# Six heads of V instead of four kept on chip, and FFN weights read in three column blocks, in a one-core decode layer with its gradients

## The chip, the cores and the metric

The kernel runs on one core of one Trainium2 chip. The core has five engines that run side by side, each with its own queue of instructions in a fixed order: TensorE (PE), VectorE (DVE), ScalarE (ACT), GpSimd (POOL) and SyncE (SP). DMA transfers are issued from the queues of SP, POOL or ACT and are carried by 16 DMA engines that all queues share. The metric is the device time of one execution in microseconds; the time before is the median of ten runs.

## What is computed

One token (x, 448 wide) passes through an attention block over a KV cache and then a gated feed-forward block (FFN). The outputs are the layer's result and the gradients of all its inputs.

```python
W = min(4096, max(256, Sk // 4))               # the last 4096 of 32768 cache rows
q = layernorm(x) @ wq                           # 16 heads of 256, 8 KV heads
k, v = k_cache[:, :, Sk-W:, :], v_cache[:, :, Sk-W:, :]
o = softmax(q @ k.T / 16) @ v
h = x + o @ wo
g, u = layernorm(h) @ w_gate, layernorm(h) @ w_up
h2 = h + (g * u) @ w_down
# outputs: h2, and d/d(x, k_cache, v_cache, wq, wo, w_gate, w_up, w_down)
```

The gradients of k_cache and v_cache have the full shape (8, 32768, 256). Rows outside the window are zero and have to be written as zeros: 112 pieces of 2 MiB in all. That is most of what the kernel writes.

## The kernel before

All working memory is one tile, `arena`, cut by hand into overlapping views (L47-85). Views with the same bytes are used at different times, and the framework turns each overlap into a wait. The framework also decides the order of instructions in each engine's queue: it may move an instruction ahead of others in the program where its inputs allow it, but on the engine the order is then fixed, so an instruction that waits holds everything behind it.

**Zero fills.** 103 transfers of 2 MiB are issued by POOL from the very start (L113-119), all from one 16 KB-per-partition buffer of zeros (`zeros`, two halves that are cleared at L87 and L88). Each fill sends 128 rows of 16,384 bytes. Eight fills are in flight at a time: the next is issued when the oldest has landed. Another 18.9 MB of zeros (`late_jobs`, L112) go out on SP's queue at the end, from a buffer that first held V (L589, L610-613).

**First loop** (L256-324), over the 8 KV heads: K and V of a head (2 MiB each, 128 rows of 16 KB) are loaded on SP's queue. `scores` transposes K and forms the softmax; `moments` scales K by the probabilities on DVE (L298), multiplies it with V (L302, into `M_sb`), and sums the attention output (L306). There are three K slots and four V slots (`HELD = 4`); after the loop, V of heads 4 to 7 is still in the slots.

**Middle.** `wo` is loaded whole once K's slots are free (L323), the FFN weights behind it (L326-328, in one piece each, rows of 10,752 and 1,792 bytes); `w_down` was loaded near the start (L194) and its products with the incoming gradient were formed in the first loop (L218). Then attention output (L347), second layernorm (L350), gate and up (L354-357), the spread of the FFN gradient over all partitions (L372-377, into `dg_bc`), products of the weights with it on DVE (L387, L390), the backward layernorm, 32 products with `wo` (L412), and the gradient of the queries, spread into `dq_bc` (L453-458).

**Second loop** (L528-608), over heads in the order 4 5 6 7 0 1 2 3: transposes of V (L243, copies L534 and L536), then the gradients of V and K, which PE forms in pieces (L574), and ACT and DVE copy into staging slots (L578-582); two stores of 2 MiB on SP's queue follow (L584). There are three staging slots, and each round takes two. V of heads 0 to 3 is loaded again in this loop (L539, L541). The weight gradients are put into `wst` buffers on DVE (`outer`, L467, and `outer_B`, L496-497) and stored on SP's queue, spread over the rounds by `plan` (L523). `wq` is loaded a second time (L543-544) and multiplied with `dq_bc` in round 5 (L593, L596), which gives the gradient of x.

A width of 448 is no multiple of 128. The kernel lays 384 rows over 128 partitions and the other 64 rows over 128 half rows (`wqA`/`wqB`, `wg_sb`/`wgB_sb`, `par_f`, `pair_f`, `half_f`).

Of the kernel before, what the change touches and what calls it, by code (L numbers as in the profile page):

```python
# [7 lines left out]
bf16 = mybir.dt.bfloat16  # L8
f32 = mybir.dt.float32
# [4 lines left out]
D = 448  # L14
H = 16
# [5 lines left out]
FH = F // 2  # L21
NB = 7
# [3 lines left out]
ZW = 8192  # L26
NZ = (Sk - W) * Dh // (128 * ZW)
HELD = 4
# [4 lines left out]
def kernel(  # L33
# [12 lines left out]

    VB = 16 * KB  # L47
    MB = VB + HELD * 16 * KB
    RB = MB + 32 * KB
    TOTAL = RB + 81 * KB + 128  # L50
# [4 lines left out]

    zeros = ar(0, ZW)
    V_slot = [ar(VB + 16 * KB * i, T * Dh).rearrange("p (t d) -> p t d", d=Dh) for i in range(HELD)]
    M_sb = [ar(MB + 4 * KB * g, 4 * KB).bitcast(f32).rearrange("p (v h d) -> p v h d", v=2, h=2) for g in range(G)]
    wqA = ar(MB, 24 * KB).rearrange("p (c j) -> p c j", c=3)
    wqB = ar(MB + 24 * KB, 4 * KB)  # L60
    K_slot = [ar(RB + o * KB, T * Dh).rearrange("p (t d) -> p t d", d=Dh) for o in (16, 32, 0)]
    KT_slot = [ar(RB + (48 + 2 * i) * KB, 2 * KB).rearrange("p (e t k) -> p e t k", t=4, e=2) for i in range(3)]
    pK_slot = [ar(RB + (54 + 4 * i) * KB, 4 * KB).rearrange("p (t h d) -> p t h d", t=4, h=2) for i in range(2)]
    wo_sb = ar(RB, 28 * KB).rearrange("p (j n) -> p j n", n=D)
    wg_sb = [ar(RB + 28 * KB + 6272 * i, 3 * F).rearrange("p (c f) -> p c f", c=3) for i in range(2)]
    wgB_sb = [ar(RB + 28 * KB + 6272 * i + 3 * F, FH) for i in range(2)]
    junk = ar(RB + 105 * KB // 2, F)
    o_rows = junk[0:H, 0:2 * Dh].bitcast(f32)
    om = junk[:, 2 * Dh:4 * Dh].bitcast(f32).rearrange("p (a j) -> p a j", a=8)
    h_row = ar(RB + 119 * KB // 2, 2 * D)[0:1].bitcast(f32)  # L70
    diag = ar(RB + 56 * KB, F)
    wd_sb = ar(RB + 62 * KB, 2 * NB * D).rearrange("p (h b n) -> p h b n", h=2, b=NB)
    dg_bc = ar(RB + 62 * KB + 6272, 2 * F).rearrange("p (i f) -> p i f", i=2)
    junk0 = ar(RB + 62 * KB + 6272, D)
    ppad = [ar(RB + 62 * KB + 6272 + 512 * (i + 1), T * H).rearrange("p (t h) -> p t h", h=H) for i in range(2)]
    rows1, rows2 = [ar(o, 2 * KB)[0:16].bitcast(f32) for o in (RB + 62 * KB + 6272 + 1536, RB + 70 * KB)]
    ok_rows = ar(RB + 62 * KB + 6272 + 2560, 2 * KB)[0:H].bitcast(f32).rearrange("p (k d) -> p k d", k=2)
    stage = [ar(RB + 16 * KB * i, T * Dh).rearrange("p (t d) -> p t d", d=Dh) for i in range(3)]
    Rbig = [ar(o, 8 * KB).rearrange("p (l n) -> p l n", l=8) for o in (RB + 48 * KB, MB + 24 * KB)]
    VT_slot = [ar(RB + (56 + 2 * i) * KB, 2 * KB).rearrange("p (e t k) -> p e t k", t=4, e=2) for i in range(3)]  # L80
    dq_bc = ar(RB + 62 * KB, H * Dh)
    Zr = ar(RB + 72 * KB, KB).rearrange("p (w k i) -> p w k i", w=4, k=32)
    wst = [ar(MB + 12 * KB * i, 12 * KB) for i in range(2)]
    wq2A = ar(VB + 2 * 16 * KB, 24 * KB).rearrange("p (c j) -> p c j", c=3)
    wq2B = ar(VB + 2 * 16 * KB + 24 * KB, 4 * KB)
# [5 lines left out]
    wq_A = A_wq[0:384, :].rearrange("(p c) j -> p c j", c=3)  # L91
    wq_B = A_wq[384:D, :].rearrange("r (h j) -> (r h) j", h=2)
    LD.dma_start(out=wqA, in_=wq_A)
    LD.dma_start(out=wqB, in_=wq_B)
# [16 lines left out]

    late_jobs = [(out_2, G - 1, 5, 7, 2 * ZW), (out_3, G - 1, 0, 6, 2 * ZW), (out_3, G - 1, 6, 7, ZW)]  # L112
    for g in range(G):  # L113
        for o in (out_2, out_3):
            if g == G - 1 and o is out_3:
                continue
            reg = zero_rows(o, g, 0, 5 if g == G - 1 else NZ, ZW)
            for i in range(reg.shape[0]):
                ZQ.dma_start(out=reg[i], in_=zeros)  # L119


    pair_f = const.tile([128, 64], f32)
    nc.vector.reduce_sum(out=pair_f[:], in_=ident_f[:].rearrange("p (m w) -> p m w", w=2), axis=AX)
    par_f = const.tile([128, 2], f32)
    nc.vector.reduce_sum(out=par_f[:], in_=ident_f[:].rearrange("p (m w) -> p w m", w=2), axis=AX)
# [8 lines left out]
    half_f = const.tile([128, 4], f32)  # L134
    nc.vector.memset(half_f[:, 0:3], 1.0)
    nc.vector.memset(half_f[:, 3:4], 0.5)
# [5 lines left out]

    def to_columns(row, dt, out_ps, name):
        dup = small.tile([1, 128], dt, tag="dup" + name, bufs=1)
        nc.vector.tensor_copy(out=dup[:].rearrange("o (m w) -> o m w", w=2), in_=row[:, 384:D].unsqueeze(2).to_broadcast([1, 64, 2]))
        one = ones_bf if dt == bf16 else ones_f
        for c in range(3):
            nc.tensor.matmul(out_ps[:, c:c + 1], lhsT=row[:, c:384:3], rhs=one[0:1, 0:1], start=True, stop=True)
        nc.tensor.matmul(out_ps[:, 3:4], lhsT=dup[:], rhs=one[0:1, 0:1], start=True, stop=True)

    def layernorm(row, dt, name):
# [6 lines left out]
        ps = ps_t.tile([128, 6], f32, tag="tmp")  # L158
        to_columns(row, dt, ps, name)
        nc.tensor.matmul(ps[:, 4:6], lhsT=ones_f[0:1, 0:128], rhs=mv[:, 0:2], start=True, stop=True)  # L160
        xc = const.tile([128, 6], f32, tag=name + "xc")
        nc.vector.tensor_copy(out=xc[:], in_=ps[:])
        xT = const.tile([128, 4], f32, tag=name + "xT")
        nc.vector.tensor_scalar(out=xT[:], in0=xc[:, 0:4], scalar1=xc[:, 4:5], scalar2=xc[:, 5:6], op0=ALU.subtract, op1=ALU.mult)
        X_b = const.tile([128, 5], bf16, tag=name + "Xb")
        nc.vector.tensor_copy(out=X_b[:, 0:3], in_=xT[:, 0:3])
        nc.vector.tensor_scalar(out=X_b[:, 3:5], in0=par_f[:], scalar1=xT[:, 3:4], scalar2=None, op0=ALU.mult)
        return xc[:, 5:6], xT, X_b

    def layernorm_bwd(dcat, xT, rstd, plus, name):  # L170

        nc.vector.tensor_tensor(out=dcat[:, 4:8], in0=dcat[:, 0:4], in1=xT[:], op=ALU.mult)
        ps = ps_t.tile([128, 2, 4], f32, tag="tmp")
        nc.tensor.matmul(ps[:].rearrange("p a b -> p (a b)"), lhsT=ones_f[:], rhs=dcat[:], start=True, stop=True)
        m = small.tile([128, 2], f32, tag="lnm")
        nc.vector.reduce_sum(out=m[:], in_=ps[:], axis=AX)
        nc.vector.tensor_scalar(out=m[:], in0=m[:], scalar1=-1.0 / D, scalar2=None, op0=ALU.mult)
        t = small.tile([128, 4], f32, tag="lnt")
        nc.vector.tensor_scalar(out=t[:], in0=xT[:], scalar1=m[:, 1:2], scalar2=m[:, 0:1], op0=ALU.mult, op1=ALU.add)
        nc.vector.tensor_tensor(out=t[:], in0=t[:], in1=half_f[:], op=ALU.mult)  # L180
        nc.vector.tensor_tensor(out=t[:], in0=t[:], in1=dcat[:, 0:4], op=ALU.add)
        r = const.tile([128, 4], f32, tag=name + "r")
# [3 lines left out]
    def load_kv(dst, cache, g):  # L186
        LD.dma_start(out=dst, in_=cache[0, g, Sk - W:, :].rearrange("(p t) d -> p t d", t=T))

    load_kv(K_slot[0], A_k_cache, 0)
    LD.dma_start(out=dh2_bc[:], in_=grad_out.rearrange("a b d -> (a b) d").to_broadcast([128, D]))  # L190
    load_kv(V_slot[0], A_v_cache, 0)
    load_kv(K_slot[1], A_k_cache, 1)
    load_kv(V_slot[1], A_v_cache, 1)
    LD.dma_start(out=wd_sb, in_=B_w_down.rearrange("(h p b) n -> p h b n", h=2, b=NB))  # L194
    load_kv(K_slot[2], A_k_cache, 2)
    load_kv(V_slot[2], A_v_cache, 2)
    load_kv(V_slot[3], A_v_cache, 3)

    rstd1, xnT_f, X1_b = layernorm(x_bf[:], bf16, "ln1")
    d2_ps = ps_t.tile([128, 4], f32, tag="tmp")  # L200
    to_columns(dh2_bc[0:1, :], bf16, d2_ps, "d2")
    d2_T = const.tile([128, 4], f32)
    nc.vector.tensor_tensor(out=d2_T[:], in0=d2_ps[:], in1=half_f[:], op=ALU.mult)
    qT_ps = ps_s.tile([128, 32], f32, tag="rows")
    for c in range(16):
        nc.tensor.matmul(qT_ps[:, c::16], lhsT=wqB[:, c * 128:(c + 1) * 128], rhs=X1_b[:, 3:5], start=True, stop=False)
        for h in range(2):
            col = 16 * h + c
            for k in range(3):
                nc.tensor.matmul(qT_ps[:, col:col + 1], lhsT=wqA[:, k, col * 128:(col + 1) * 128], rhs=X1_b[:, k:k + 1],  # L210
                                 start=False, stop=(h == 1 and k == 2))
    qT_bf = const.tile([128, 32], bf16)
    nc.vector.tensor_copy(out=qT_bf[:], in_=qT_ps[:])

    d_hh = const.tile([128, 2, NB], f32)
    for h in range(2):
        for b in range(NB):
            nc.vector.tensor_tensor_reduce(out=junk0, in0=wd_sb[:, h, b, :], in1=dh2_bc[:], scale=1.0, scalar=0.0,  # L218
                                           op0=ALU.mult, op1=ALU.add, accum_out=d_hh[:, h, b:b + 1])
# [33 lines left out]
    with tc.tile_pool(name="ps_m", bufs=1, space=bass.MemoryType.PSUM) as ps_m, \  # L253
# [4 lines left out]
        def scores(g):  # L258
            fill_vpad(g % 2, qT_bf[:, 4 * g:4 * g + 4].rearrange("p (k e) -> p e k", e=2))
            sT_ps = dots(K_slot[g % 3], KT_slot, vpad[g % 2], rows1, ps_c, "cols", lambda q, XT, ps: nc.scalar.copy(out=XT, in_=ps))  # L260
# [29 lines left out]
        def moments(g, p_f):  # L290
            K_sb, V_sb = K_slot[g % 3], V_slot[g % HELD]
# [18 lines left out]

        ok_ps = ps_x.tile([H, 2, Dh], f32, tag="ok")
        p_next = scores(0)
        for g in range(G):
            p_f = p_next
            if g + 1 < G:
                p_next = scores(g + 1)
            moments(g, p_f)
            if g + 3 < G:
                load_kv(K_slot[g % 3], A_k_cache, g + 3)
            if g + HELD < G:  # L320
                load_kv(V_slot[g % HELD], A_v_cache, g + HELD)
            if g == G - 2:
                LD.dma_start(out=wo_sb, in_=A_wo.rearrange("(p j) n -> p j n", j=32))  # L323
# [6 lines left out]
    with tc.tile_pool(name="ps_mid", bufs=3, space=bass.MemoryType.PSUM) as ps_mid, \  # L330
# [31 lines left out]
        for i in range(2):  # L362
            nc.vector.tensor_tensor(out=dgu_f[:, i], in0=d_hh[:], in1=gu_f[:, 1 - i], op=ALU.mult)
# [279 lines left out]
```

## Time and profile before

| what | value |
|---|---|
| median of 10 runs | 815.92 us (810.53 to 823.71) |
| the profiled execution | 814.14 us, of which the profile's span is 812.1 us |
| mean granted TensorE clock | 0.759 of full speed |
| PE / DVE / ACT busy | 452.2 / 366.1 / 192.8 us |
| DMA traffic | 339.01 MB, mean 417 GB/s |
| fills on POOL's queue (q0) | 103 transfers, 216.01 MB |
| all loads and other stores (q1) | 122.48 MB |
| end of the first loop's last product (L306) | 312.1 us |
| last two stores of the second loop issued (L584) | 758.7 us |

How to read what follows: a page of the profile gives busy shares by engine and by slice of the span, the DMA queues, and the costliest groups of instructions. A group's line has its source line, engine, operation, output<-input, count, then busy time and mean duration in ns, then the idle time before it and what ended it. A line of waits gives the waiting engine and line, what it waited for, the total in us, how often, and the longest. A line of the timeline gives start and duration in us. The trace also holds a record of each DMA packet (one row moved by one DMA engine) with its size, queue, start and duration. "Fill 42" is the 42nd of the 103 fills on POOL's queue.

### The profile page before, as it was taken

To read this page: it belongs to the slowest core of one execution; us is meant where nothing else is said; L and a number is where in the kernel's file an instruction comes from. 1 tells how busy PE (TensorE), PEld (TensorE's weight loads), DVE (VectorE), ACT (ScalarE), POOL (GpSimd) and SP (SyncE) were. 2 spreads that over 40 slices of the span, in tenths; PEclk is the share of its full clock that TensorE was granted. 3 is DMA by queue.
4 is the path that set the end of the run, shared out by engine and by line. 5 is a ranking of instruction groups with operands and counts; after the bars stand their busy time and mean duration, and the time that the engine had idled before them with its cause. 6 is when DMAs were issued, how large, how long until landed. Compare 5 with 4: busy or idle time off the path is not lost.

```text
span 812.1 us, 8341 instructions
## 1 busy us (share of the span) xinstructions
PE 452.2 (56%) x3128; PEld 244.2 (30%) x3151; DVE 366.1 (45%) x1153; ACT 192.8 (24%) x301; POOL 60.7 (7%) x112
## 2 busy tenths in 40 slices
PE   0455999999999998430664834842331155120100
PEld 0332445455456455210552412420110032000000
DVE  2022753634624752298424834563466265352200
ACT  0142043242232201110010614332031054141200
POOL 4000000000001100111101000000000000000000
PEclk9978899999999999565695976565665586655555
DMA  9999999999999999999999999999999999999994
GB/s 356 427 430 429 431 429 428 430 431 427 432 422 429 427 414 416 427 431 431 424 424 423 409 425 428 399 433 416 426 417 415 431 428 434 419 431 426 429 434 178
DMA packets 24366, 339.01 MB, mean 417 GB/s; under 512 B 2691, under 2 KB 3334, under 8 KB 4358
## 3 DMA queue, kind: packets, MB, share of 16 engines
q0 software_dynamic: 14832, 216.01, 63.0%
q1 hardware_dynamic: 9494, 122.48, 35.8%
q8 instruction: 24, 0.39, 0.2%
q14 instruction: 16, 0.13, 0.0%
HBM read 57.89 MB, written 280.59 MB: 417 GB/s over the span
## 4 chain that ended last, share of the span: by engine, by line
DMA 29%; DVE 10%; PE 8%; ACT 2%; issue 1%; another core or an unknown queue 1%; SPq 0%; DVEq 0%; ACTq 0%
DMA out_dram<-arena 29%; DVE arena L412 2%; PE d_ps L574 2%; DVE arena L581 2%; PE rows_ps L246 2%; DVE arena L582 2%; PE tr_ps L243 1%; PE dqb_ps L453 1%; ACT arena L579 1%; DVE arena L467 1%; ACT arena L534 1%; DVE arena L387 1%; DVE arena L566 0%; PE dqb_ps L456 0%
## 5 line engine op out<-in xcount | busy, mean ns | idle before, releaser
L298 DVE TENSOR_SCALAR arena<-arena,p_f 128x256 bf16<-128x256 bf16 x512 | 109.5, 281 | 64.4 <-PE M_ps L302 35.1
L574 PE MATMUL d_ps<-arena,rT 32*128 32x512 bf16 x256 | 41.5, 509 | 158.1 <-ACT arena L579 111.6
L302 PE MATMUL M_ps<-arena 128*128 128x512 bf16 x489 | 122.0, 384 | 1.3 <-issue 0.2
L243 PE MATMUL tr_ps<-ident_bf,arena 128*128 128x128 bf16 x1024 | 89.6, 240 | 34.5 <-DVE arena L536 17.5
L119 POOL DMA_DIRECT2D out_dram<-arena x103 | 56.2, 546 | 653.6 <-DMA out_dram<-arena 653.6
L246 PE MATMUL rows_ps<-arena,vpad 128*16 128x512 bf16 x256 | 86.8, 439 | 22.3 <-DVE arena L536 15.4
L243 PEld LDWEIGHTS <-arena 128*128 128x128 bf16 x1024 | 67.8, 108 | 70.2 <-issue 60.7
L582 DVE CAST arena<-d_ps 128x512 bf16<-128x512 f32 x64 | 43.6, 681 | 84.5 <-DMA out_dram<-arena 84.5
L260 ACT COPY arena<-tr_ps 128x1024 bf16<-128x1024 bf16 x64 | 61.7, 1015 | 81.6 <-PE tr_ps L243 81.6
L574 PEld LDWEIGHTS <-rT 32*128 32x128 bf16 x256 | 10.9, 95 | 180.9 <-issue 141.2
L579 ACT CAST arena<-d_ps 128x512 bf16<-128x512 f32 x64 | 38.0, 593 | 106.3 <-DMA out_dram<-arena 106.3
L302 PEld LDWEIGHTS <-arena 128*128 128x128 bf16 x512 | 46.0, 99 | 51.8 <-issue 8.2
L306 PE MATMUL ok_ps<-arena 128*16 128x256 bf16 x512 | 59.9, 277 | 1.1 <-DVE arena L287 0.9
L578 ACT CAST arena<-d_ps 128x512 bf16<-128x512 f32 x64 | 37.6, 588 | 68.6 <-PE d_ps L574 68.4
L581 DVE CAST arena<-d_ps 128x512 bf16<-128x512 f32 x64 | 43.9, 685 | 20.3 <-PE d_ps L574 20.1
L306 PEld LDWEIGHTS <-arena 128*16 128x16 bf16 x512 | 45.3, 91 | 16.7 <-issue 5.9
L534 ACT COPY arena<-tr_ps 128x1024 bf16<-128x1024 bf16 x32 | 32.5, 1014 | 55.5 <-PE tr_ps L243 51.5
L246 PEld LDWEIGHTS <-vpad 128*16 128x16 bf16 x256 | 19.8, 92 | 71.2 <-issue 63.2
L309 ACT COPY arena<-M_ps 128x512 f32<-128x512 f32 x16 | 8.6, 589 | 82.4 <-PE M_ps L302 82.4
L536 DVE COPY arena<-tr_ps 128x1024 bf16<-128x1024 bf16 x32 | 21.8, 683 | 3.6 <-PE tr_ps L243 3.6
L467 DVE TENSOR_SCALAR arena<-arena,xT 128x1792 bf16<-128x1792 bf16 (+1 forms) x9 | 8.0, 886 | 31.2 <-DMA out_dram<-arena 19.9
L412 DVE CUSTOM_DVE_ANT_0 arena<-arena,dh_bc 128x448 bf16<-128x448 bf16 x32 | 20.0, 624 | 1.1
(184 smaller groups left out, 334.6 us busy)
## 6 DMA issues: line engine op xcount, KB each, us to landing
out_dram<-arena POOLq DMA_DIRECT2D x103, 2048.0 KB, 59.4
out_dram<-arena SPq DMA_DIRECT2D x17, 2048.0 KB, 27.5
arena<-in_A_v_cache_dram SPq DMA_DIRECT2D x12, 2048.0 KB, 36.8
arena<-in_A_k_cache_dram SPq DMA_DIRECT2D x8, 2048.0 KB, 21.1
out_dram<-arena SPq DMA_DIRECT2D x4, 4096.0 KB, 42.0
arena<-in_A_wq_dram SPq DMA_DIRECT2D x2, 3072.0 KB, 13.3
arena<-in_A_wo_dram SPq DMA_DIRECT2D x1, 3584.0 KB
out_dram<-arena SPq DMA_DIRECT2D x3, 1024.0 KB, 44.0
```

What stands on the lines that cost most here:

```text
L119: ZQ.dma_start(out=reg[i], in_=zeros)
L243: nc.tensor.transpose(tr_ps[:, dh, i, :], X_sb[:, 4 * q + i, dh * 128:(dh + 1) * 128], ident_bf[:])
L246: nc.tensor.matmul(rows_ps[:], lhsT=pad[:, dh, 16 * q:16 * q + 16], rhs=XT[:, dh].rearrange("p t k -> p (t k)"), start=(q == 0 and dh == 0 ...
L260: sT_ps = dots(K_slot[g % 3], KT_slot, vpad[g % 2], rows1, ps_c, "cols", lambda q, XT, ps: nc.scalar.copy(out=XT, in_=ps))
L298: nc.vector.tensor_scalar(out=pK[:, i, hh, :], in0=K_sb[:, t, :], scalar1=p_f[:, 8 * i + c, hh:hh + 1], scalar2=None, op0=ALU.mult)
L302: nc.tensor.matmul(M_ps[:, vh, :], lhsT=V_sb[:, t, vh * 128:(vh + 1) * 128], rhs=pK[:, i, :, :].rearrange("p h d -> p (h d)"), start=(t == ...
L306: nc.tensor.matmul(ok_ps[:, k, :], lhsT=ppad[g % 2][:, 8 * (t % 4) + t // 4, :], rhs=X_sb[:, t, :], start=(g == 0 and k == 0 and t == 0), ...
L534: nc.scalar.copy(out=XT, in_=ps)
L574: nc.tensor.matmul(d_ps[:, qi].rearrange("p w d -> p (w d)"), lhsT=rT[32 * q:32 * (q + 1), :], rhs=RB_[32 * q:32 * (q + 1), l, :], start=T ...
L579: nc.scalar.copy(out=stK[:, t:t + 2, :], in_=d_ps[:, :, 1, :])
L581: nc.vector.tensor_copy(out=stV[:, t:t + 2, :], in_=d_ps[:, :, 0, :])
L582: nc.vector.tensor_copy(out=stK[:, t:t + 2, :], in_=d_ps[:, :, 1, :])
```

## The change

The 448 rows are now laid over 112 partitions, four rows each (`DP = 112`, `DC = 4`), for `wq`, the gate and up weights and their gradients; the half-row views and their helpers go. The arena gets smaller behind V: six V slots, 32 KB for M, 50 KB for the rest. K2 is put where `wq` was, K5 and V7 into the slot of V1, V6 into that of V0.

- The second loop runs 2 3 4 5 6 7 0 1 and loads V of heads 0 and 1 alone again, into the space of `M_sb`, right after `dq_bc` is formed. The gradient of V is written over V itself (`stV = V_sb`); that of K has two staging slots.
- `wo` is loaded in two halves, the second after the first loop.
- Gate, up and down weights are loaded in three blocks of 640, 512 and 640 columns. Gate and down are issued by SP, up by ACT. Blocks 0 and 2 use one place, block 1 the upper half of the zero buffer. Each block is worked through to its products before the next; block 2 is loaded when block 0 is done.
- Fills 1 to 42 are as before. Fills 43 to 63 read the lower half of the zero buffer twice (256 rows of 8 KB). After block 1 the upper half is cleared again on DVE, and fills 64 to 103 follow as before.
- The second load of `wq` and its products (four of 112x4096) stand ahead of the second loop. `dg_bc` is formed again in the second loop (`expand_dg`) for the gradients of gate and up.

```diff
-HELD = 4
+DP = 112
+DC = 4
+BLOCKS = [(0, 5), (640, 4), (1152, 5)]
+HALF0, HALF1 = 42, 63
...
+    A_off = [VB + 16 * KB * i for i in range(6)]
+    V_off = [A_off[i] for i in (0, 1, 2, 3, 4, 5, 0, 1)]
+    K_off = [RB, RB + 16 * KB, MB + 16 * KB, RB, RB + 16 * KB, A_off[1], RB, RB + 16 * KB]
+    wgu_off = [RB + 28 * KB, ZW // 2]
+    wd_off = [RB + 38 * KB, RB + 38 * KB + 5 * D]
+    wq2 = ar(RB, 32 * KB)[0:DP].rearrange("p (c j) -> p c j", c=DC)
+    Rbig = [ar(RB + 8 * KB * i, 8 * KB).rearrange("p (l n) -> p l n", l=8) for i in range(2)]
+    dK_off = [RB + 16 * KB, A_off[2]]
+    wst = [ar(A_off[3 + i], 16 * KB) for i in range(2)]
...
+    def send_fills(n0, n1, halves=False):
+        for reg in fills[n0:n1]:
+            if halves:
+                ZQ.dma_start(out=reg.rearrange("p (k f) -> p k f", k=2), in_=zeros[:, 0:ZW // 2].unsqueeze(1).to_broadcast([128, 2, ZW // 2]))
+            else:
+                ZQ.dma_start(out=reg, in_=zeros)
+    send_fills(0, HALF0)
+    send_fills(HALF0, HALF1, True)
...
+        after = {0: [("K", 3), ("V", 3)], 1: [("K", 4), ("V", 4), ("K", 5)], 2: [("V", 5)], 3: [("V", 6), ("K", 6)], 4: [("K", 7)], 5: [("V", 7)]}
...
+    def load_block(n):
+        f0, nb, w, wgu, wd = block_views(n)
+        for eng, i, wt in ((LD, 0, B_w_gate), (nc.scalar, 1, B_w_up)):
+            eng.dma_start(out=wgu[:, :, i, :], in_=wt.rearrange("(p c) f -> p c f", c=DC)[:, :, f0:f0 + w])
+        LD.dma_start(out=wd, in_=B_w_down[f0:f0 + w, :].rearrange("(p b) n -> p b n", b=nb))
+    load_block(0)
+    load_block(1)
...
+        for n in range(len(BLOCKS)):
+            for b in range(nb):
+                nc.vector.tensor_tensor_reduce(out=dgb[:, 0:D], in0=wd[:, b, :], in1=dh2_bc[:], scale=1.0, scalar=0.0,
+                                               op0=ALU.mult, op1=ALU.add, accum_out=d_hh[:, b0 + b:b0 + b + 1])
...
+            for c in range(DC):
+                nc.vector.tensor_tensor_reduce(out=wc, in0=wc, in1=dgb[0:DP, 0:2 * w], scale=1.0, scalar=0.0,
+                                               op0=ALU.mult, op1=ALU.add, accum_out=dhn[:, c, n:n + 1])
+            if n + 2 < len(BLOCKS):
+                load_block(n + 2)
+            if n == 1:
+                nc.vector.memset(ar(ZW // 2, ZW // 2), 0.0)
+                send_fills(HALF1, len(fills))
...
+        LD.dma_start(out=wq2, in_=wq_v)
...
+        for g in range(2):
+            load_kv(MB + 16 * KB * g, A_v_cache, g)
+        for c in range(DC):
+            nc.vector.tensor_tensor_reduce(out=wq2[:, c, :], in0=wq2[:, c, :], in1=dq_bc[0:DP], scale=1.0, scalar=0.0,
+                                           op0=ALU.mult, op1=ALU.add, accum_out=dcat1[:, c:c + 1])
...
+        plan = [[], [], [job_o(0)], [job_o(1)], [job_d, job_q(0)], [expand_dg, job_q(1), job_g(0)], [job_g(1)], []]
+        order = [2, 3, 4, 5, 6, 7, 0, 1]
-            if it < 2:
-                load_kv(V_slot[it], A_v_cache, order[HELD + it])
-            elif it in (HELD, HELD + 1):
-                load_kv(V_slot[it % 2], A_v_cache, order[it + 2])
-            stV, stK = stage[stc % 3], stage[(stc + 1) % 3]
+            stV, stK = V_sb, kv_at(dK_off[it % 2])
```

## The prediction

> **What bounds the kernel now.** I read the page first: engines, slices, queues, bytes.
>
> ```profile
> PE 452.2 (56%) x3128; PEld 244.2 (30%) x3151; DVE 366.1 (45%) x1153; ACT 192.8 (24%) x301; POOL 60.7 (7%) x112
> ...
> DMA  9999999999999999999999999999999999999994
> ...
> q0 software_dynamic: 14832, 216.01, 63.0%
> q1 hardware_dynamic: 9494, 122.48, 35.8%
> ...
> HBM read 57.89 MB, written 280.59 MB: 417 GB/s over the span
> ```
>
> No engine is busy above 56%, but the DMA engines are busy in every slice but the last, and the two queues fill 98.8% of their time. The kernel is as long as its transfers. An edit gains what it takes off the DMA engines and loses only where it leaves them without work. Compute matters where stores come too late to be carried beside something else; so the waits come next.
>
> ```profile
> POOL out_dram L119 <- DMA out_dram<-arena: 653.6, 95, 11.8
> ...
> ACT arena L579 <- DMA out_dram<-arena: 106.3, 7, 23.2
> DVE arena L582 <- DMA out_dram<-arena: 84.5, 7, 18.0
> ```
>
> POOL always has a fill ready, and in the second loop ACT and DVE wait for stores: compute waits for DMA, not the reverse. SP's timeline gives the end of that loop:
>
> ```profile
> 660.62 1.64 SPq L584 DMA_DIRECT2D out_dram<-arena  x2
> ...
> 758.66 1.63 SPq L584 DMA_DIRECT2D out_dram<-arena  x2
> ```
>
> The fifth and the eighth pair of stores are shown, three rounds apart. Behind the last one, at 758.7 us, come two late zero jobs behind it (with the pair 4.19 + 6.29 MB, 25 us at 417 GB/s); the transfers end at 812. So about 28 us of other traffic still lay ahead: the second loop has that much slack.
>
> **The terms on the DMA engines.** The trace's packet records give medians of 611 ns for a row of 16,384 bytes, 309 for 8,192, 159 for 4,096, 74 for 1,792 and 41 for 896: 8 ns plus bytes over 27.2 bytes/ns, loads and stores alike. All is divided by 16 engines.
>
> ```profile
> arena<-in_A_v_cache_dram SPq DMA_DIRECT2D x12, 2048.0 KB, 36.8
> ```
>
> - V: 12 loads become 10. Two loads are 256 rows at 613 ns (mean of q1's rows of that size): 156.9 us / 16 = -9.8.
> - Gate and up: 512 rows become 2,688 of 1,280 and 1,024 bytes, same bytes: 2,176 x 8 ns / 16 = +1.1.
> - Fills 43 to 63: 21 x 128 rows more, x 8 ns / 16 = +1.3.
> - The other layouts: `wq` twice, its gradient and those of gate and up have 288 rows fewer each (-864), w_down and its gradient 128 more each, `wo` 128 more, its gradient 128 fewer: -608 rows in all, -0.3.
>
> Sum -7.7. The 112-partition transfers carry 17.4 MB (`wq` twice 7.3, its gradient 3.7, gate and up and their gradients 6.4), 42 us at 417 GB/s. No transfer of before has 112 partitions. Bounds from the rows of weights: `wq`'s first load took 1,069 ns a row in the mean against a median of 921 (+16%), the 10,752-byte rows 407 against 404 (+1%); a gain isn't excluded either, since 1% is the spread. So -0.4 to +6.7; I take 0, as the 10,752-byte rows are the nearest.
>
> [...]
>
> **The waits that the change adds, and what covers them.** Fills are the cover. In POOL's timeline:
>
> ```profile
> 267.13 0.54 POOL L119 DMA_DIRECT2D out_dram<-arena  x1 [4.56 <-DMA out_dram<-arena]
> ...
> 318.47 0.53 POOL L119 DMA_DIRECT2D out_dram<-arena  x1 [6.16 <-DMA out_dram<-arena]
> ...
> 388.20 0.53 POOL L119 DMA_DIRECT2D out_dram<-arena  x1 [4.36 <-DMA out_dram<-arena]
> ...
> 432.96 0.53 POOL L119 DMA_DIRECT2D out_dram<-arena  x1 [5.91 <-DMA out_dram<-arena]
> ```
>
> These are fills 42, 50, 63 and 71. Eight are in flight, so fill 42 landed near 318 and fill 63 near 433.
>
> *Block 1's load* waits for fill 42. On SP stand w_down's block 1 and later loads behind it, on ACT the second layernorm's root and all copies. The first loop's last product ends at 312; the wait is some 6 us, and block 0 is being worked through meanwhile: nothing.
>
> *Fill 64* waits for the clearing after block 1; 39 fills stand behind it on POOL. My estimate of the middle: second half of `wo` issued at 312, landed by 321; block 0's rows alternate one for one with fill rows (while 128 rows of 1,792 bytes went out on SP's queue, 324.6 to 330.9, POOL's sent some 160): 28 per engine at 309 + 55 + 55 ns = 11.7, w_down 8 x (309 + 174) = 3.9, so 337 for block 0 and 353 for block 1. A block's work is 5 products (0.62, L412's kind), small steps of some 6 us, and four products of 1,280 columns (L387's 2.02 us by 1,280/1,792: 1.44), about 15 us. Block 0 is done at 352, block 1 near 368, block 2 (its load waits on SP and ACT for block 0, `wq`'s second load behind it; 353 to 369) near 384; before, L390 ended at 363.7. So the middle grows by 20 us, 10 to 40. The clearing comes near 368, 65 us ahead of 433, when the DMA engines would run dry. Nothing; without cover each us costs one.
>
> [...] The alternation says the small rows on two queues take two turns of three (11.7 us a block, against 56 x 364 ns = 20.4 on one); but both lie beside fills, so the sum is the same either way.
>
> *Second loop.* L412 (21 us), the query gradient and its copies shift by 20: `dq_bc` complete near 439 instead of 419. `wq`'s second load starts behind the last L412 (411) and lands by 431 at half the rate; V of heads 0 and 1 behind it is needed in round 6. Then four products stand on DVE ahead of the loop:
>
> ```profile
> L593 DVE CUSTOM_DVE_ANT_0 arena<-arena 128x4096 bf16<-128x4096 bf16 x3 | 13.3, 4420 | 5.1 <-DMA arena<-in_A_wq_dram 5.1
> ```
>
> 4 x 4.42 = 18 us, so 457; the first pair of stores leaves near 475 (466.5 before). SP then carries 4.2 MB of stores a round and at most 5.3 of weight gradients, no V until round 6, so its half share is enough for rounds of about 33 us: the three rounds between the lines above took 32.7 each, waits for staging slots among it. K's gradient waits for the store two rounds back, in round 1 for V's store one round back; buffers of `wst` for stores one to three rounds back, with DVE's rest behind. Seven rounds of 33 end at 706; if all DVE work for weight gradients is added (some 31 us, of which 9 for the second forming of `dg_bc`), at 737. Traffic ends near 804. The moved steps cost nothing; the stores' stalls that go are worth nothing either, since fills took that time.
>
> **Sum.** 812.1 - 7.7 = 804.4 of span, 806.5 against the execution's 814.14. That execution was 1.8 below the median of ten, 815.92; so 808 for the median. What a measurement of this kernel can tell from no change is 0.3%, 2.4 us.
>
> **The rivals.**
> - *The gain is eaten by rows* (no change). The 112-partition transfers at +16%: -7.7 + 6.7 = -1.0, 815. For: `wq`'s first load; against: all else in the records. Chance 8%.
> - *The second loop sets the end* (slower). With the late zero jobs all behind the last stores, 23.1 MB or 55 us follow these: they must leave by 749; with two jobs behind, by 777. From 475 that is a pace of 39 to 43 us; above it each us of pace costs seven. The first four gaps were 48.5 in the mean (466.5 to 660.6): 475 + 340 = 815 for the last stores, and 842 to 870 for the end; 842, since before put late jobs between the stores. For: DVE's order is fixed, so a weight job that waits for a store holds its copies. Against: those four gaps held reloads of V and more jobs. Chance 7%.
> - *Block 1 comes late* (slower). If up's load is put early in ACT's queue (a memset of L438 ran at 4.1 us and L440 at 25.7, far ahead of their places, and L218 held DVE for 9.0 us), ACT stops in the first loop until fill 42 lands, and block 1 passes 433. 40 us late: -7.7 + 15 in dry time, 823. Chance 4%.
> - *The loads don't go*: 12 V loads would show. Under 1%.
>
> **How the numbers follow.** The forecast, 801 to 813, has 80%. The range 801 to 818 takes in the first rival. Faster 0.82 (the forecast, and 2 of the first rival's 8, at half its price), same 0.08 (the other 6, the loads that don't go, and 1 of a slow rival's mild case), slower 0.10 (the slow rivals' other 10).
>
> **What would show it.** Ten V loads, under 335 MB, DMA at 9 in all slices but the last; no wait of POOL (fill 64) beyond 12 us; last stores before 750. Wrong if a slice near 430 or after 700 falls below 9, or if rows of 1,280 bytes take more than 60 ns.

## The result and the profile after

The changed kernel takes 822.79 us (median of 15 runs, 819.49 to 825.86). The kernel before, run beside it 53 times, takes 816.2. The ratio is 1.0094, 95% interval [1.0068, 1.012]: slower by 0.9%. The forecast was 808 with a range up to 818; both were wrong. The profiled execution has a span of 821.6 us at a granted clock of 0.758, the clock of before.

Of the page of the changed kernel: the engines, the DMA engines by slice, what they moved, the queues, and two groups of transfers (count, KB each, median us from issue to landing).

```profile
PE 449.3 (55%) x3170; PEld 243.0 (30%) x3193; DVE 364.9 (44%) x1149; ACT 196.0 (24%) x309; POOL 63.3 (8%) x112
...
DMA  9999999999999999999999999999999999999993
GB/s 298 431 428 430 431 429 428 430 430 428 421 428 424 418 422 411 423 422 428 428 343 430 432 428 431 426 426 427 426 424 427 318 390 417 318 414 429 433 419 157
...
q0 software_dynamic: 17520, 216.01, 62.8%
q1 hardware_dynamic: 9366, 116.68, 35.3%
...
HBM read 53.69 MB, written 280.59 MB: 407 GB/s over the span
...
arena<-in_A_v_cache_dram SPq DMA_DIRECT2D x10, 2048.0 KB, 41.9
...
arena<-in_A_wq_dram SPq DMA_DIRECT2D x2, 3584.0 KB, 19.5
```

Read the DMA line and the GB/s line one under the other. The engines are as busy as before, in every slice but the last, and 4.19 MB less is read. But they move 407 GB/s instead of 417. The GB/s line of the kernel before:

```profile
GB/s 356 427 430 429 431 429 428 430 431 427 432 422 429 427 414 416 427 431 431 424 424 423 409 425 428 399 433 416 426 417 415 431 428 434 419 431 426 429 434 178
```

The loss isn't spread out: it lies in slices 1, 21, 32, 33 and 35. Slice 1 is low in before as well (356), but between the first slice and the last before has no such dips (its lowest is 399). The same stretches in the windows of both kernels (columns: stretch, length, five engines, PE clock, DMA share, GB/s); first before, then after:

```profile
412.00:432.00 20.00, 7.63 (x45) 6.24 (x44) 6.04 (x16) 2.69 (x4) 1.75 (x3) 0.78 1.01 424
632.00:662.00 30.00, 14.21 (x110) 6.80 (x110) 14.06 (x37) 11.01 (x19) 2.13 (x4) 0.67 1.01 429
690.00:730.00 40.00, 9.25 (x64) 3.14 (x61) 18.18 (x39) 12.11 (x22) 1.62 (x3) 0.58 1.01 430
```

```profile
412.00:432.00 20.00, 19.26 (x106) 16.72 (x106) 2.26 (x13) 4.00 (x6) 0.90 (x2) 0.86 1.01 344
632.00:662.00 30.00, 15.31 (x113) 6.99 (x113) 17.72 (x37) 11.62 (x20) 1.61 (x3) 0.65 1.02 338
690.00:730.00 40.00, 4.88 (x32) 0.96 (x28) 11.96 (x23) 8.69 (x16) 1.60 (x3) 0.50 1.00 359
```

In the changed kernel these are the stretches of the second `wq` load, the stores of its gradient, and the stores of the gate and up gradients: transfers over 112 partitions. The packet records price it. Each packet's duration is set against 8 ns + bytes / 27.17 bytes/ns (the prediction's fit, with one more digit: a row of 16,384 bytes then takes the median of 611 ns); what is above is called excess. All per DMA engine (sum / 16), in us:

| | before | after | difference |
|---|---|---|---|
| packets by the fit | 792.2 | 784.5 | -7.6 |
| excess | 12.2 | 28.3 | +16.2 |
| no packet in the record | 7.8 | 8.8 | +1.0 |
| span | 812.1 | 821.6 | +9.5 |

The first row is the prediction's sum, -7.7. The second is the term that it took as 0. Rows of 32,768 bytes in the `wq` loads took 1,851 and 1,633 ns in the mean, against 1,220 for the same size in stores over 128 partitions. In the stores of the gate and up gradients rows of 14,336 bytes took 755 in the mean, against a median of 535 for that size, and in those of `wq`'s gradient rows of 16,384 bytes took 900 against 611. The fills beside them suffered too: beside the second `wq` load their 8,192-byte rows took 407 ns in the mean, where the median of all is 309.

### The profile page after: what moved, and what is told of

The parts are those of the page before. It is cut to its first block, busy times and chain, and to the rows that moved or that the text cites. A ratio compares the mean times of both kernels' runs of the same rounds, so it can differ in the third digit from the quotient of the medians.

```text
span 821.6 us, 8438 instructions
## 1 busy us (share of the span) xinstructions
PE 449.3 (55%) x3170; PEld 243.0 (30%) x3193; DVE 364.9 (44%) x1149; ACT 196.0 (24%) x309; POOL 63.3 (8%) x112
## 2 busy tenths in 40 slices
DMA packets 28318, 334.83 MB, mean 408 GB/s; under 512 B 2643, under 2 KB 5462, under 8 KB 6230
## 4 chain that ended last, share of the span: by engine, by line
another core or an unknown queue 43%; DMA 39%; issue 4%; POOL 3%; POOLq 0%
DMA out_dram<-arena 39%; POOL out_dram L129 3%; POOL out_dram L127 0%; POOLq L613 0%; POOL ident_bf masks.py:199 0%; POOL ident_f masks.py:199 0%; POOL ident_bf masks.py:197 0%; POOL ident_f masks.py:197 0%; POOL arena L93 0%; POOLq L602 0%
## 5 line engine op out<-in xcount | busy, mean ns | idle before, releaser
L230 PE MATMUL tr_ps<-ident_bf,arena 128*128 128x128 bf16 x1024 | 87.5, 235 | 16.7 <-ACT arena L536 8.4
L129 POOL DMA_DIRECT2D out_dram<-arena x82 | 44.8, 547 | 558.0 <-DMA out_dram<-arena 547.2
L230 PEld LDWEIGHTS <-arena 128*128 128x128 bf16 x1024 | 65.8, 105 | 67.1 <-issue 57.8
L289 PEld LDWEIGHTS <-arena 128*128 128x128 bf16 x512 | 46.2, 99 | 50.9 <-issue 6.5
L293 PE MATMUL ok_ps<-arena 128*16 128x256 bf16 x512 | 57.5, 273 | 0.9 <-DVE arena L274 0.9
L464 DVE CUSTOM_DVE_ANT_0 arena<-arena 112x4096 bf16<-112x4096 bf16 x4 | 17.5, 4421 | 23.4 <-ACT arena L458 23.4
L127 POOL DMA_DIRECT2D out_dram<-arena x21 | 14.0, 669 | 111.3 <-DMA out_dram<-arena 111.3
```

The costliest lines, as they stand in the source:

```text
L129: ZQ.dma_start(out=reg, in_=zeros)
L230: nc.tensor.transpose(tr_ps[:, dh, i, :], X_sb[:, 4 * q + i, dh * 128:(dh + 1) * 128], ident_bf[:])
L289: nc.tensor.matmul(M_ps[:, vh, :], lhsT=V_sb[:, t, vh * 128:(vh + 1) * 128], rhs=pK[:, i, :, :].rearrange("p h d -> p (h d)"), start=(t == ...
L293: nc.tensor.matmul(ok_ps[:, k, :], lhsT=ppad[g % 2][:, 8 * (t % 4) + t // 4, :], rhs=X_sb[:, t, :], start=(g == 0 and k == 0 and t == 0), ...
```

## The experiments

Theory A: transfers over 112 partitions hold the DMA engines longer. Theory B: it is where the loads and stores now stand, not their shape. In e1_all128 and the kernels built on it, the 448 rows are cut into 128 equal pieces instead of 112; the bytes are the same.

**e1_all128, e2_loads128, e3_stores128.**

```diff
-    LD.dma_start(out=wq_sb, in_=wq_v)
+    LD.dma_start(out=ar(MB, 28 * KB), in_=wq_flat)      # 128 x 28,672 bytes
...
-        LD.dma_start(out=wq2, in_=wq_v)
+        LD.dma_start(out=ar(RB, 28 * KB), in_=wq_flat)
...
-  LD.dma_start(out=(out_6, out_7)[i].rearrange("(p c) f -> p (c f)", c=DC), in_=buf[0:DP, 0:DC * F])
+  LD.dma_start(out=(out_6, out_7)[i].rearrange("r f -> (r f)").rearrange("(p x) -> p x", p=128), in_=buf[:, 0:D * F // 128])
...
-  LD.dma_start(out=out_4.rearrange("(p m c) j -> p m (c j)", m=2, c=2)[:, n, :], in_=buf[0:DP, 0:2 * H * Dh])
+  LD.dma_start(out=out_4.rearrange("r j -> (r j)").rearrange("(m p x) -> m p x", m=2, p=128)[n], in_=buf[:, 0:14 * KB])
```

e1 has all four edits, e2 the first two (the loads), e3 the last two (the stores).

> The changed kernel, but wq's two loads and the stores of the gradients of wq, gate and up move the same bytes over 128 partitions (28,672, 14,336 and 12,544 bytes a partition) instead of 112; the arrangement on chip no longer fits the computation, so q, the gradient of x and those three weight gradients are not the reference's. Theory A (transfers over 112 partitions slow the DMA engines): the row excess of some 16 us goes, so about 822 - 16 = 806, ratio to the kernel before 0.986 to 0.991. Theory B (the excess comes from where the transfers stand: the wq load ahead of the loop, weight stores late and together): still 818 to 823, ratio above 1.002.

> The changed kernel with wq's two loads alone over 128 partitions (q and the gradient of x are not the reference's). Theory A: the excess around the two loads (about 4.7 and 4.2 us) falls to that of the kernel before (1.7 and 1.3): 6 us less, about 816.5, ratio 1.000. Theory B: no change, 1.007 to 1.012.

> The changed kernel with the stores of the gradients of wq, gate and up alone over 128 partitions (those three outputs are not the reference's). Theory A: the excess of 7.3 and 6.6 us around these stores falls to about 2 in all: 11 to 12 us less, about 811, ratio 0.994 to 0.997. Theory B: no change, 1.007 to 1.012.

| | us | ratio to before, 95% interval | excess, us per DMA engine |
|---|---|---|---|
| e1_all128 | 801.59 | 0.9815 [0.9739, 0.9892] | 10.3 |
| e2_loads128 | 817.33 | 1.0013 [0.9972, 1.0055] | 22.8 |
| e3_stores128 | 807.88 | 0.9895 [0.9818, 0.9972] | 15.1 |
| after | 822.79 | 1.0094 [1.0068, 1.012] | 28.3 |

The windows of e1_all128, same stretches:

```profile
412.00:432.00 20.00, 19.86 (x102) 17.11 (x103) 1.63 (x12) 4.00 (x6) 1.07 (x2) 0.80 1.01 410
632.00:662.00 30.00, 16.47 (x121) 7.48 (x121) 19.00 (x39) 12.65 (x21) 2.83 (x4) 0.67 1.02 428
690.00:730.00 40.00, 4.40 (x28) 0.86 (x27) 10.66 (x18) 8.10 (x15) 1.07 (x2) 0.50 1.01 428
```

The order of the work is that of the changed kernel, and the dips are gone. Theory B falls. The shape is worth 21 us of time and 18.0 of excess; taken alone the loads are worth 5.5 us of excess, the stores 13.2. e1 and e3 came out faster than theory A said (801.59 against 806, 807.88 against 811). It had counted the excess alone, and the time without packets fell too: from 8.8 us to 5.3 in e1 and 6.5 in e3.

**e4_before112**, the other way round: the kernel before with its second `wq` load and the stores of the three gradients over 112 partitions, in their old places (dx and these three gradients are not the reference's then).

```diff
-  LD.dma_start(out=ov[0:384, :].rearrange("(p c) f -> p (c f)", c=3), in_=buf[:, 0:3 * F])
+  LD.dma_start(out=ov.rearrange("(p c) f -> p (c f)", c=4)[:, 0:3 * F], in_=buf[0:112, 0:3 * F])
...
-  LD.dma_start(out=out4_A[:, c, :], in_=buf[:, 0:H * Dh])
+  LD.dma_start(out=out_4.rearrange("(p c) j -> p c j", c=4)[:, c, :], in_=buf[0:112, 0:H * Dh])
```

> The kernel before, with V of four heads and all else as it was, but the second load of wq and the stores of the gradients of wq, gate and up over 112 partitions (the gradients of x, wq, gate and up are not the reference's). Theory A: about +3 us for the load and +8 to +12 for the stores, so 827 to 831, ratio 1.013 to 1.018. Theory B: the transfers stand where they stood, so 0.998 to 1.002.

829.63 us, ratio 1.0156 [1.007, 1.0243]; the excess rises from 12.2 to 23.5 us. Its GB/s line has the dips at the places of before's own `wq` load and stores:

```profile
GB/s 356 429 429 430 429 430 430 428 428 429 430 424 428 428 414 419 430 432 429 393 393 389 411 427 429 363 428 422 378 418 364 433 421 428 426 426 428 426 403 81
```

In the mean, rows of 8,192 bytes took 411 to 436 ns, of 10,752 bytes 547 to 573, of 32,768 bytes 1,543; the medians over 128 partitions are 309, 404 and 1,220. That is 26 to 42% more, and two of these lengths are before's own, so the longer rows of the new layout aren't the cause. The means hide a wide spread: of the first 224 rows of 8,192 bytes 161 stayed within 3% of the fit, and 32 took more than twice as long.

**e5_split and e9_evenodd.** Is it the number 112, or which partitions are named? Both keep e1's rows but issue the second `wq` load and the `wq`-gradient stores as two transfers of 64 partitions: e5 the lower and the upper 64, e9 the even and the odd ones. (The gate and up gradients: 96 + 32 in e5, even and odd in e9.)

```diff
-        LD.dma_start(out=ar(RB, 28 * KB), in_=wq_flat)
+        for s in range(2):                                    # e5
+            LD.dma_start(out=ar(RB, 28 * KB)[64 * s:64 * s + 64], in_=wq_flat[64 * s:64 * s + 64])
...
+        for s in range(2):                                    # e9
+            LD.dma_start(out=ar(RB, 28 * KB)[s:128:2], in_=wq_flat[s:128:2])
```

> The kernel e1_all128 (801.59 us; all transfers over 128 partitions, so that q, dx and the three weight gradients of wq, gate and up are not the reference's) with the same bytes in the same rows, but the second wq load and the two wq-gradient stores issued as two transfers of 64 partitions each, and the gate/up-gradient stores as 96 + 32. Theory A1, that a row's engine is set by its position in the transfer and rows slow down where two engines meet on the same group of partitions: 64 rows give four to an engine, so two engines share every group of eight partitions, and the excess comes back: rows of 28,672 bytes at 1,300 to 1,900 ns instead of 1,060 to 1,100, span 808 to 820. Theory A2, that only an uneven share of rows (112 of 128) matters: every count here is a multiple of 16, as 112 is, so each engine has the same number of rows, and the time stays at 801 to 803.

> e5_split with another choice of partitions: the same loads and stores are issued as two transfers of 64 partitions each, but the even and the odd ones instead of the lower and the upper half (gate and up gradients too). If engine e gets rows 4e to 4e+3 of a transfer, these now lie on partitions 8e to 8e+7, as in a transfer over 128, and no two engines meet on a group of eight. Theory A1 (it is the meeting on a group of eight partitions): the excess goes, 801 to 805, rows of 28,672 bytes near 1,120 ns, of 14,336 near 545. Theory A3 (a transfer over fewer than 128 partitions is slow in itself): as e5_split, 818 to 824, rows of 28,672 bytes near 1,690, of 14,336 near 930.

e5: 822.39 us, ratio 1.0063 [1.003, 1.0097], excess 29.9. e9: 806.86 us, ratio 0.9863 [0.9793, 0.9934], excess 10.4. The stretch of the `wq` load (done at 433 us in e5, at 424 in e9), first e5, then e9:

```profile
412.00:432.00 20.00, 20.00 (x106) 17.40 (x105) 0.70 (x6) 4.06 (x7) 0.53 (x1) 0.85 1.02 288
```

```profile
412.00:432.00 20.00, 6.54 (x36) 5.08 (x37) 3.49 (x15) 1.01 (x1) 1.07 (x2) 0.53 1.00 417
```

Same bytes, same rows, same number of transfers: 288 GB/s for halves, 417 for every second partition (row means 1,688 and 1,117 ns; 14,336-byte rows 929 and 544). Theory A2 (only an uneven share counts) and A3 (fewer than 128 is slow in itself) both fall. What counts here is which rows a transfer takes together, halves or every second one. A1 gave e9's row times (near 1,120 and 545 ns), and missed its 801 to 805 us by 2. Its mechanism, that DMA engines meet on the same partitions, is not shown: no record here names the engine or the partition of a row. Nor do the runs separate the partition from the place in DRAM, since each row keeps both in e1, e5 and e9. A row pitch in DRAM isn't enough by itself: the late zero stores have a pitch of 32,768 bytes, like the `wq` loads, and over 128 partitions their rows take 1,219 ns. e9's remaining 5 us over e1 are not excess: SP's last four stores left only from 770.33 on, two slices at the end run at 339 and 215 GB/s, and the time without packets is 9.2 us against 5.3.

**e6_vtwice and e7_onequeue**: terms of the prediction, tested on e1. In e6 V of heads 0 and 1 is loaded twice; in e7 the up blocks go out on SP's queue.

```diff
-            load_kv(MB + 16 * KB * g, A_v_cache, g)
+            for _ in range(2):                                # e6
+                load_kv(MB + 16 * KB * g, A_v_cache, g)
...
-        for eng, i, wt in ((LD, 0, B_w_gate), (nc.scalar, 1, B_w_up)):
+        for eng, i, wt in ((LD, 0, B_w_gate), (LD, 1, B_w_up)):   # e7
```

> e1_all128 with V of heads 0 and 1 loaded twice into the same place (4.19 MB more, nothing else; the outputs are e1_all128's). If the prediction's V term is right, the two loads cost 2,048 rows of 8,192 bytes a 16th each by the engine's measured time, 9.8 us: 811.4 us, ratio to the kernel before 0.990 to 0.995. Rival: the loads were hidden anyway and the gain of 18.7 us in e1_all128 comes from elsewhere: 801 to 803.

> e1_all128 with the up-weight blocks issued on SP's queue like the gate blocks, instead of ACT's. The prediction costs the second queue at nothing: 800 to 803. Rival: the second queue takes a share from the fills or brings the blocks earlier: block 0 lands more than 5 us later and the time is 805 or more.

e6: 811.28 us, 9.7 above e1 (ratio to before 0.994 [0.9905, 0.9974]). The V term of 9.8 is right. (The expectation's 2,048 rows are a slip: two V loads are 256 rows of 16,384 bytes, which give its 9.8 us.) e7: 801.76 us, 0.9816 [0.9767, 0.9866]: 0.2 us beside e1's 801.59, so the second queue is worth nothing either way.

**e8_rows128**: the whole change, but with `wq`, its gradient and the gate and up gradients in before's layout (three rows to a partition, and 64 rows as half rows). The FFN blocks stay 112 wide.

```diff
+    wq_A = A_wq[0:384, :].rearrange("(p c) j -> p c j", c=3)
+    wq_B = A_wq[384:D, :].rearrange("r (h j) -> (r h) j", h=2)
+    LD.dma_start(out=wqA, in_=wq_A)
+    LD.dma_start(out=wqB, in_=wq_B)
...
+                LD.dma_start(out=ov[0:384, :].rearrange("(p c) f -> p (c f)", c=3), in_=buf[:, 0:3 * F])
+                LD.dma_start(out=ov[384:D, :].rearrange("r (h f) -> (r h) f", h=2), in_=buf[:, 3 * F:3 * F + F // 2])
```

> The changed kernel with wq, its gradient and the gate and up gradients again in the layout of the kernel before (three rows to a partition, and 64 rows as half rows, over 128 partitions); the FFN weight blocks keep 112 partitions. It computes all of the reference. Theory A (transfers over 112 partitions slow the engines): the sum of the prediction without its 112-partition term holds, less what the FFN blocks still cost: 800 to 808 us, ratio 0.978 to 0.990. Theory B (placement of the loads and stores): 815 or more.

It takes 802.5 us, ratio 0.9826 [0.9776, 0.9876]: faster than both kernels. Its page:

```profile
GB/s 353 430 429 431 429 428 430 430 429 429 429 423 423 429 418 403 421 421 427 428 425 414 425 429 429 426 425 425 427 424 425 424 427 420 424 423 430 429 434 191
...
HBM read 53.69 MB, written 280.59 MB: 417 GB/s over the span
```

The rate of before, with 4.19 MB less. The 112-wide FFN blocks show no such loss: their rows of 1,280 and 1,024 bytes took 55 to 56 and 46 ns in the mean, where the fit gives 55 and 46, and the slices of their loads (15 and 16) run at 418 and 403. So 112 partitions don't slow rows of every length; why the short ones are spared stays open, and A1 doesn't say it.

**e10_before and e11_before**: two more profiles of the kernel before, whose times spread over 811 to 826 us while e8's lie within 801.9 to 804.3.

> The kernel before, unchanged, for a second profile: its times spread over 810 to 828 us, those of e8_rows128 over 801.9 to 804.3. If this execution is one of the long ones (over 818), theory A says its packets show the extra time as longer rows in one stretch; the rival says that it is time without packets.

> The kernel before, unchanged, for a third profile, with the expectations of e10_before.

They took 821.47 and 814.55 us. The long one doesn't come from longer rows: its excess is 12.4, against 12.2 in the first profile of before (span 812.1) and 10.4 in e11. All its packets together take 804.6, against 804.3 and 802.5. The rival holds for most of it: of the 6.7 us over the first profile 6.4 are time without packets (14.2 against 7.8), of the 6.0 over e11 3.9 (14.2 against 10.2). It lies at the end. The GB/s lines of e10 and e11, with 65 and 125 in the last slice:

```profile
GB/s 357 428 429 429 430 427 431 428 429 420 430 421 428 428 407 425 429 431 426 422 425 420 411 429 418 418 426 418 430 407 429 430 430 427 426 427 432 427 408 65
```

```profile
GB/s 356 429 430 428 432 428 428 430 428 423 428 422 430 424 413 423 426 430 429 426 422 422 410 432 424 419 430 427 429 423 432 427 435 425 429 422 433 429 427 125
```

The 16 engines don't finish together. In e10 the number that are busy falls from 16 at 794 us to none at 813.5, when the last row has gone: 19 us. In e11 this takes 13 us, in the first profile of before 12. From the last row to the end of the span it is another 5.4, 5.5 and 3.0 us. Why the same program ends more unevenly in one execution than in another stays open.

## Why the prediction was wrong, point by point

- **What bounds the kernel**: right. The DMA engines are busy in all slices but the last (the page has 9 tenths or more), and the times follow what each experiment did to the packets. The exceptions are time without packets: e9's last stores left late, and in e10 the end is uneven.
- **V -9.8, small rows, half fills, other layouts; sum -7.7**: right. Packets by the fit fell by 7.6, e6 gives 9.7 for V, rows of 1,280, 1,024 and 8,192 bytes have medians of 55, 46 and 309 ns.
- **The 112-partition transfers, "I take 0"**: this step failed, in value and in bounds. It measures +16.2 in the excess against before, 18.0 against e1. The bounds -0.4 to +6.7 came from rows that all went over 128 partitions, so none of them had the shape that it is about. The upper one also rests on a misreading: 1,069 ns is the mean of both `wq` loads, and the first alone took 1,126 against the median of 921 (+22%, which would have made +9.3, still too little). "The 10,752-byte rows are the nearest" chose nearness by length; over 112 partitions (e4) rows of that length take 547 to 573 ns in the mean. And the price was put on the transfer's own rows alone, while the fills beside it took longer too (407 ns a row of 8,192 bytes beside the second `wq` load, against 309): of the 18.0 us, 5.5 are in POOL's queue.
- **Block 1 and fill 64**: right. Fill 64 went out at 397.32 after the usual wait of 4.53 us. (The 128 rows of 1,792 bytes from which the alternation was read went out from 321.6 to 328.0 in before, beside 144 fill rows: 3 us earlier than the prediction has it, and still about one for one.) The longer waits of POOL in this stretch come later, with the `wq` load:

```profile
397.32 0.55 POOL L129 DMA_DIRECT2D out_dram<-arena  x1 [4.53 <-DMA out_dram<-arena]
...
411.83 0.53 POOL L129 DMA_DIRECT2D out_dram<-arena  x1 [4.40 <-DMA out_dram<-arena]
426.31 0.53 POOL L129 DMA_DIRECT2D out_dram<-arena  x1 [13.94 <-DMA out_dram<-arena]
439.63 0.53 POOL L129 DMA_DIRECT2D out_dram<-arena  x1 [12.79 <-DMA out_dram<-arena]
```

- **The middle and the products of `wq`**: the four products run from 438.5 to 455.9 (forecast 439 to 457). First stores at 484.4 (475), the last between 706 and 737 as forecast. SP's timeline in the changed kernel:

```profile
685.66 1.78 SPq L578 DMA_DIRECT2D out_dram<-arena  x2
687.49 1.56 SPq L588 DMA_DIRECT2D out_dram<-arena  x1
726.27 2.81 SPq L578 DMA_DIRECT2D out_dram<-arena  x2
729.13 4.13 SPq L588 DMA_DIRECT2D out_dram<-arena  x3
```

- **Rivals**: "eaten by rows" named the right term, at under half its price, and so stood on the wrong side of no change. The second loop did not set the end, block 1 was not late, the loads went (ten).
- **What would show it**: nearly every sign asked for came true (ten loads, 334.83 MB, DMA at 9, fill 64 after 4.53 us, rows of 55 ns, last stores before 750), and the kernel was slower. POOL's waits don't tell either: some later fills waited longer than the 12 us set for fill 64, up to 17.65 in the changed kernel, but up to 13.86 in the fast e1 too. The signs watched whether the engines are busy; the DMA line reads 9 in slice 21 of both kernels, where rows moved at 424 GB/s before and at 343 after. The GB/s line would have told.
- **From 808 to e8's 802.5**: against before's profile e8's packets by the fit fall by 7.2, its excess by 2.0 and its time without packets by 1.7: 10.9 of span. The medians, 816.2 and 802.5, lie 13.7 apart. The other 3 us may be the uneven end of before, which its own profiled execution (814.14) had little of; only one long execution, e10, shows it.

## What to carry to other kernels

Where DMA bounds, price a re-layout by the partitions that a transfer names too, not by bytes and rows alone: here 448 rows as 112 x 4 cost 20 us that 384 + 64 half rows over 128 partitions did not (822.79 against 802.5), though the short rows of the FFN blocks over 112 partitions cost nothing (55 to 56 ns for 1,280 bytes, 55 by the fit). If a change brings a shape that no row of the trace has, rows of another shape don't bound it; leave the range open on that side, or keep the shape. Read the busy line and the GB/s line together: busy at a lower rate was the sign of slow rows (343 GB/s in slice 21, `wq`'s rows at 1,633 ns in the mean).

## What was not expected of the hardware

- Over 112 partitions rows of 8,192 to 32,768 bytes took 26 to 47% longer in the mean (the first `wq` load, whose rows are long over 128 partitions too, 1,126 ns against a median of 921 in before, is left out of this), though many single rows took the usual time (in e4 161 of the first 224 rows of 8,192 bytes were within 3% of the fit); rows of 1,280 and 1,024 bytes took no longer (55 to 56 and 46 ns, 55 and 46 by the fit). Fill rows beside the second `wq` load took 407 ns in the mean, against a median of 309.
- Two `wq` transfers of 64 partitions, with the fills beside them, ran at 417 GB/s when they took every second partition and at 288 when they took halves.
- The number of DMA engines at work fell from 16 to none in 19 us in one execution of the kernel before (e10), which is 6 to 7 us longer than two others with the same packets, where it took 12 and 13.
